# q, k and v handed over feature-on-partitions: no transposes of them on the chip, and a new order of the front

## The chip, the cores and the metric

One core of a Trainium2 chip runs the whole program. The metric is device time in microseconds (us), the median of several runs. TensorE (PE) does the matrix products, VectorE (DVE), ScalarE (ACT) and GpSimd (POOL) the elementwise work, SyncE (SP) issues every load and store from one queue.

## The reference, cut to what matters

```python
# q, k, v: (2, 8, 576, 64) float32; w_in 512x1024, w_out 1024x512, w1, w2: four experts; inputs of w_* are float64
mask_plain = (rel >= 0) & (rel < 32)                              # heads 0-3
mask_dil = (rel >= 0) & (rel < 128) & (rel % 4 == 0)              # heads 4-7
attn = softmax(where(mask, q @ k.T / 8, -1e9)); x = (attn @ v) as (1152, 512)
h = x @ w_in; solu = h * softmax(h); x = layernorm(solu) * g_ln @ w_out
out = sum over 4 experts of p[:, e] * (relu(x @ w1[e]) @ w2[e])
```

## The kernel before, in words

The program has two parts. The **front** computes the attention and the first layer; its order is written out as a table of tokens, `ORDER`, and each token runs a Python generator to its next `yield`, so the table sets the order of instructions on every engine (a `+` moves the step's copy or subtraction to another engine). The **loop** behind the table computes the experts and is the same for all kernels here.

The tokens of the front:

- `lI`, `VI`: load of a 128-row block of `w_in` (float64, as pairs of integers) and its conversion to a high and a low float32 part (`convert`, `conv_in`), five or six steps on ACT, DVE and POOL; `lO`, `VO` the same for `w_out`.
- `lD`, `lP`: loads of q and k with positions on partitions, for the dilated heads (4-7) and the plain heads (0-3). `AD`, `AP` (`att_AD`, `att_AP`): TensorE transposes of them into PSUM and copies to `qTd`, `kTd`, `qTp`, `kTp`, with features on partitions. `lvd`, `lvp` load v.
- `UD`, `UP` (`att_U`): a unit of attention, 96 positions of four dilated heads or 192 of four plain ones; three units of each kind for each of two batches, so twelve. In a unit PE writes mask and scores (L307, L318), DVE and ACT do the softmax, PE transposes the probabilities (L343), a copy brings them to `pt`, PE multiplies with v (L357), and a copy and a subtraction write the result's high and low parts `xhi`, `xlo`.
- `H.t` (`moe_H`): token tile t (0 to 8) times `w_in`, 24 matmuls of 512 columns in one go (L386), then the softmax-like function; `T.t` (`moe_T`) transposes its result (L413); `X.c.dp` (`moe_X`) multiplies a third of the tokens with half of `w_out`, 48 matmuls (L433).
- `WP`, `XQ`, `WV`: preparation of the experts' weights and inputs by additions and high/low splits; `u`, `d` the first products of the experts (L545, L615).

PSUM has four tiles: `pm` (two buffers; for `H`, `X` and most of `AD`, `AP`) and `pa` (two; for the units and `T`). The queue of each engine is executed in order, so a waiting instruction holds what stands behind it.

Of the kernel before, what the change touches and what calls it, by code (L numbers as in the profile page):

```python
# [8 lines left out]
F32 = mybir.dt.float32  # L9
BF16 = mybir.dt.bfloat16  # L10
# [37 lines left out]
def fused_kernel(ctx, tc, q, k, v, w_in, w_out, g_ln, probs, w1, w2, out):  # L48
    nc = tc.nc
    B, H, S, D = q.shape  # L50
# [45 lines left out]
    warmb = ap1.tile([128, 224], BF16, name="warmb", tag="warmb")
    nc.vector.memset(warmb, 0.0)
    nc.vector.memset(kTd[:, :, 0:32], 0.0)
    nc.vector.memset(kTp[:, :, 0:32], 0.0)
    nc.vector.memset(vd[0:32, 0], 0.0)  # L100
# [29 lines left out]
    def load_qk(quad, u, b):  # L130
        for nm, src in (("q", q), ("k", k)):
            if quad == "D":
                h0 = 4 + 2 * u
                t = rdp.tile([72, 2, 8 * D], F32, name=f"rd{nm}", tag=f"rd{nm}")
                nc.sync.dma_start(out=t, in_=src[b, h0:h0 + 2].rearrange("h (p r) d -> p h (r d)", r=8))
            else:
                s0 = TH * u
                t = ap2.tile([96, 2, 4, D], F32, name=f"rp{nm}", tag=f"rp{nm}")
                nc.sync.dma_start(out=t, in_=src[b, 0:4, s0:s0 + TH].rearrange("h (p r) d -> p r h d", r=2))
            raws[nm, quad, u, b] = t  # L140

    def load_vd(b):
        vr = v[b, 4:8].rearrange("h (i r j) d -> r i h (j d)", r=2, j=2)
        for c in range(3):
            x = max(96 * c - 32, 0)
            while x < 96 * c + 96:
                r, i = divmod(x, 144)
                n = min(144 - i, 96 * c + 96 - x)
                p = x - (96 * c - 32)
                nc.sync.dma_start(out=vd[p:p + n, c], in_=vr[r, i:i + n])  # L150
                x += n
# [14 lines left out]
    fill = [0]  # L166

    def busy(ps):
        for _ in range(fill[0]):
            nc.tensor.matmul(ps[:, 1, 288:512], lhsT=warmb[:, 0:128], rhs=warmb, start=True, stop=True)  # L170
# [87 lines left out]
    qT = {}  # L258
    cnt = [0]

    def att_AD(u, b):
        if ("D", b) not in qT:
            qT["D", b] = ap1.tile([128, 4, S // 2], F32, name="qTd", tag="qTd")
        for nm, dst in (("q", qT["D", b]), ("k", kTd[:, :, 32:])):
            raw = raws.pop((nm, "D", u, b))
            pa = ptile(True)
            busy(pa)
            for rp in range(4):
                for hd in range(2):
                    o = 144 * hd + 72 * (rp % 2)  # L270
                    nc.tensor.transpose(pa[:, rp // 2, o:o + 72], raw[:, hd, 2 * D * rp:2 * D * rp + 2 * D], ident[:72, :72])
            yield
            copy(dst[:, 2 * u:2 * u + 2].rearrange("d h (x e) -> d e h x", e=2), pa[:, :, 0:288].rearrange("d e (h x) -> d e h x", h=2))
            if nm == "q":
                yield

    def att_AP(t, b):
        qt = ap2.tile([128, 2, TH], F32, name="qTp", tag="qTp")
        qT["P", t, b] = qt
        s0 = TH * t  # L280
        for nm, dst in (("q", qt), ("k", kTp[:, :, 32 + s0:32 + s0 + TH])):
            pa = ptile(b == 0)
            busy(pa)
            raw = raws.pop((nm, "P", t, b))
            for hp in range(2):
                for r in range(2):
                    o = (2 * hp + r) * 96
                    nc.tensor.transpose(pa[:, 0, o:o + 96], raw[:, r, 2 * hp:2 * hp + 2].rearrange("p j d -> p (j d)"), ident[:96, :96])
            yield
            copy(dst.rearrange("d h (p r) -> d h r p", r=2), pa[:, 0, 0:384].rearrange("d (h r p) -> d h r p", h=2, r=2))  # L290
            if nm == "q":
                yield
# [461 lines left out]
```

## Time and profile before

| | before |
|---|---|
| median of 3 runs | 562.73 us (561.83 to 563.07) |
| the profiled execution | 561.9 us |
| its span, first to last instruction | 560.1 us |
| busy share of the span | PE 95%, DVE 65%, ACT 35%, POOL 34% |
| moved by DMA | 35.79 MB |

The profile divides the span into stretches and tells how long each engine was busy in each. A busy PE is one with a matmul in flight, not one at its peak.

### The profile page before, as it was taken

The page shows a single profiled execution, that of the slowest core. Times are in us where ns is not written, and L with a number is a line of the kernel's source. Part 1 is how long each engine was busy: PE and PEld are TensorE (multiplying, and loading weights), DVE is VectorE, ACT ScalarE, POOL GpSimd, SP SyncE. Part 2 cuts the span into 40 slices and gives each one's busy share as a digit, 9 for nine tenths or more (in the row PEclk, how much of TensorE's full clock was granted, in tenths as well). Part 3 has the DMA queues.
Part 4 walks back from the last instruction along what each step waited for, and adds up shares of the span by engine and source line. Part 5 has one row for each costly group of instructions (what it writes and reads, how often), then busy time and mean ns, then how long its engine had stood idle before and what let it go on. Part 6 is the DMA issues. An engine that isn't in the chain of part 4 may idle for free.

```text
span 560.1 us, 9023 instructions
## 1 busy us (share of the span) xinstructions
PE 533.2 (95%) x3772; PEld 479.6 (86%) x3772; DVE 365.1 (65%) x472; ACT 197.5 (35%) x309; POOL 191.6 (34%) x143
## 2 busy tenths in 40 slices
PE   2888989999999899999999999999999999999997
PEld 1667877988999889898898989989889898998986
DVE  4997889617579988476558547537645854854542
ACT  3666666415325234142142223214224322321300
POOL 3463131000063463074147127307413812730300
PEclk9999999999999999999999999999999999999999
DMA  8984262000023500040030003004004000100022
GB/s 250 286 212 112 85 158 57 1 1 1 1 77 96 179 27 1 0 152 0 1 133 18 1 19 132 1 1 151 2 1 133 18 1 4 72 0 1 1 75 94
DMA packets 33944, 35.79 MB, mean 64 GB/s; under 512 B 18800, under 2 KB 21872, under 8 KB 33520
## 3 DMA queue, kind: packets, MB, share of 16 engines
q1 hardware_dynamic: 33904, 35.22, 21.1%
q8 instruction: 29, 0.48, 0.3%
q14 instruction: 11, 0.09, 0.1%
HBM read 32.86 MB, written 2.36 MB: 63 GB/s over the span
## 4 chain that ended last, share of the span: by engine, by line
PE 84%; DVE 8%; ACT 3%; issue 2%; DMA 1%; SPq 1%; DVEq 0%; ACTq 0%
PE pa L615 18%; PE pm L615 17%; PE pm L545 15%; PE pa L545 15%; PE pm L386 9%; PE pm L433 6%; PE pa L357 2%; DMA draw<-in_moe_w_in_dram 1%; PE pa L413 1%; DVE xol L464 1%; PE pa L343 1%; PE pa L318 1%; DVE hl L464 1%; ACT pt L184 1%; DVE cva L206 1%
## 5 line engine op out<-in xcount | busy, mean ns | idle before, releaser
L558 DVE SCALAR_TENSOR_TENSOR hl<-ct,hh 128x512 fp32r<-128x512 f32 (+1 forms) x64 | 63.2, 1005 | 33.3 <-ACT hh L556 33.2
L556 ACT ACTIVATE hh<-ct 128x512 fp32r<-128x512 f32 (+1 forms) x64 | 42.2, 682 | 59.7 <-DVE ct L588 29.7
L545 PE MATMUL pm<-xoh,hh 128*128 128x256 f32 (+1 forms) x192 | 56.9, 296 | 1.1 <-DVE ct L588 1.1
L615 PE MATMUL pm<-wh,hh 128*128 128x512 f32 (+1 forms) x148 | 56.9, 384 | 0.6 <-DVE xf L620 0.6
L545 PE MATMUL pm<-xol,hh 128*128 128x256 f32 (+1 forms) x192 | 56.9, 297 | 0.3 <-DVE xol L464 0.3
L545 PE MATMUL pa<-xoh,hh 128*128 128x256 f32 (+1 forms) x192 | 56.9, 296 | 0.0
L545 PE MATMUL pa<-xoh,hl 128*128 128x256 f32 (+1 forms) x192 | 56.8, 296 | 0.0
L545 PE MATMUL pm<-xoh,hl 128*128 128x256 f32 (+1 forms) x192 | 56.8, 296 | 0.0
L545 PE MATMUL pa<-xol,hh 128*128 128x256 f32 (+1 forms) x192 | 56.8, 296 | 0.0
L615 PE MATMUL pm<-wl,hh 128*128 128x512 f32 (+1 forms) x148 | 56.8, 384 | 0.0
L615 PE MATMUL pm<-wh,hl 128*128 128x512 f32 (+1 forms) x148 | 56.7, 383 | 0.0
L615 PE MATMUL pa<-wh,hh 128*128 128x512 f32 x144 | 56.2, 390 | 0.1
L615 PE MATMUL pa<-wl,hh 128*128 128x512 f32 x144 | 56.1, 390 | 0.0
L615 PE MATMUL pa<-wh,hl 128*128 128x512 f32 x144 | 56.0, 389 | 0.0
L464 POOL TENSOR_TENSOR wl<-wl,wh 128x1024 fp32r<-128x1024 f32 x8 | 19.3, 2412 | 96.6 <-ACT wh L184 95.4
L620 DVE SCALAR_TENSOR_TENSOR xf<-pm,pr,xf 128x512 f32<-128x512 f32 (+1 forms) x33 | 24.1, 730 | 32.9 <-PE pm L615 32.9
L620 DVE SCALAR_TENSOR_TENSOR xf<-pa,pr,xf 128x512 f32<-128x512 f32 x31 | 23.1, 745 | 29.4 <-PE pa L615 29.4
L184 ACT CAST wh<-wl 128x1024 fp32r<-128x1024 f32 x15 | 15.8, 1053 | 71.0 <-PE pa L615 40.6
L464 POOL TENSOR_TENSOR hl<-sw,hh 128x512 fp32r<-128x512 f32 x20 | 30.4, 1520 | 27.8 <-ACT hh L184 27.8
L545 PEld LDWEIGHTS pm<-xoh,hh 128*128 128x128 f32 x192 | 36.4, 190 | 1.6 <-issue 1.3
L572 POOL TENSOR_TENSOR ct<-ct,ct 128x512 f32<-128x512 f32 (+1 forms) x15 | 22.3, 1484 | 45.0 <-ACT ct L570 45.0
L545 PEld LDWEIGHTS pm<-xol,hh 128*128 128x128 f32 x192 | 36.4, 190 | 0.8 <-DVE xol L464 0.5
(219 smaller groups left out, 1323.3 us busy)
## 6 DMA issues: line engine op xcount, KB each, us to landing
wl<-in_moe_w_dram SPq DMA_DIRECT2D x16, 512.0 KB, 3.9
cvr<-in_moe_w_out_dram SPq DMA_DIRECT2D x8, 512.0 KB, 3.7
rw<-in_moe_w_dram SPq DMA_DIRECT2D x8, 512.0 KB
wh<-in_moe_w_dram SPq DMA_DIRECT2D x8, 512.0 KB, 6.0
draw<-in_moe_w_in_dram SPq DMA_DIRECT2D x3, 1024.0 KB, 8.6
out_dram<-xf SPq DMA_DIRECT2D x8, 256.0 KB, 2.0
vp<-in_v_dram SPq DMA_DIRECT2D x10, 128.0 KB, 3.8
rpq<-in_q_dram SPq DMA_DIRECT2D x6, 192.0 KB, 7.1
```

Source lines behind the costliest of these rows:

```text
L184: nc.scalar.copy(out, in_)
L206: pick().tensor_tensor(out=au, in0=au, in1=low.bitcast(U32), op=ALU.add)
L357: nc.tensor.matmul(po[64 * row:64 * row + 64, 0, o:o + 96], lhsT=vv, rhs=pt[:, j, :, g, :], start=True, stop=True)
L386: nc.tensor.matmul(pm[:, n, :], lhsT=xx[:, kk, cols], rhs=ww["in", kk][:, 512 * n:512 * n + 512], start=(kk == 0 and i < 2), stop=(kk == K ...
L433: nc.tensor.matmul(pm[:, dd, 0:CW], lhsT=w_, rhs=x_[:, f, :], start=(f == 0 and i == 0), stop=(f == KF - 1 and i == 2))
L464: pick().tensor_tensor(out=out, in0=a, in1=b, op=op)
L545: nc.tensor.matmul(ps[:, ff, 0:n], lhsT=a[:, kk, fc], rhs=b[:, kk, :], start=kk == 0 and m == 0, stop=kk == 1 and m == 2)
L556: nc.scalar.activation(out=hv, in_=src, func=AF.Relu)
L558: nc.vector.scalar_tensor_tensor(out=lv, in0=src, scalar=0.0, in1=hv.bitcast(F32), op0=ALU.max, op1=ALU.subtract)
L572: poolv().tensor_tensor(out=c12, in0=c21, in1=c22, op=ALU.add)
L615: nc.tensor.matmul(po[:, u, 0:dn], lhsT=h_[:, f, cols], rhs=w_, start=(f == 0 and i == 0), stop=(f == 3 and i == 2))
L620: nc.vector.scalar_tensor_tensor(out=acc[:, t, dc], in0=po[:, u, 0:dn], scalar=pr[:, t, e:e + 1], in1=acc[:, t, dc], op0=ALU.mult, op1=ALU ...
```

## The change: layouts from outside, and what is done with the time

The host now hands over q and k with 128 partitions of features (two heads, or two of four interleaved positions, times 64) as `qp`, `kp`, `qd`, `kd`, and v with all heads of a position in one row as `vp`, `vd`. `att_AD` and `att_AP` are gone with their transposes and copies; the loads write `qTp`, `kTp`, `qTd`, `kTd` directly. These tiles and `vd` exist twice now, one set for each batch. `moe_H` yields after each quarter (the first two tiles), half or whole of its matmuls (`HCUT`), and `moe_X` after a half or the whole (`XCUT`), with its two output blocks interleaved, so that the table can put units between the pieces. The table `ORDER` is another one throughout. The computation, the loop behind the table and the number of matmuls of every kind beside the transposes of q and k are unchanged.

```diff
+KORD = (0, 1, 2, 3)
+HCUT = (1, 1, 2, 2, 4, 2, 4, 4, 4)
+XCUT = (2, 2, 4)
 ORDER = """
-lI.0 VI.0 lI.3 VI.0 lP.0.0 lD.1.0 AP.0.0 AP.0.0 VI.0 AD.1.0 VI.3 VI.3 lI.4 VI.3 AP.0.0 VI.3 VI.4 VI.4 lD.0.0 VI.3 AP.0.0 lP.1.0 lI.1 UP.0.0 AD.1.0
+lI.0 lP.0.0 VI.0 VI.0 VI.0 UP.0.0 lI.1 lD.0 VI.0 lI.4 VI.1 UP.0.0 UP.0.0 lP.1.0 UD.0.0 VI.0 VI.1 VI.1 UP.1.0 VI.1 VI.0+ VI.4 UP.0.0 VI.4 UD.0.0 UD.0.0
...
+    for b, p in enumerate((erp, ap1)):
+        kTp.append(p.tile([128, 2, 32 + S], F32, name=f"kTp{b}", tag=f"kTp{b}"))
...
+    def load_qk(quad, t, b):
+        if quad == "D":
+            nc.sync.dma_start(out=qTd[b], in_=qd[b])
+            nc.sync.dma_start(out=kTd[b][:, :, 32:], in_=kd[b])
+        else:
+            s0, s1 = (0, TH) if t == 0 else (TH, S)
+            nc.sync.dma_start(out=qTp[b][:, :, s0:s1], in_=qp[b, :, :, s0:s1])
+            nc.sync.dma_start(out=kTp[b][:, :, 32 + s0:32 + s1], in_=kp[b, :, :, s0:s1])
...
-    def att_AD(u, b):
...
-    def att_AP(t, b):
...
-        for kk in range(KD):
+        for n_, kk in enumerate(KORD):
...
+            if n_ % HCUT[t] == HCUT[t] - 1:
+                yield
...
+        for j in range(KF // 2):
+            for f in (2 * j, 2 * j + 1):
+                for dd in range(2):
...
+            if j % XCUT[c] == XCUT[c] - 1:
+                yield
```

The queue of SP at the start of the program. Before, behind a half block of `w_in` (0.52 MB), stands this; `draw` is a block of `w_in`, `rpq`, `rdq` are raw q, `rpk`, `rdk` raw k:

```order
L218 DMA draw_180<-in_moe_w_in_dram 128x1024
L139 DMA rpq<-in_q_dram 96x8x64
L139 DMA rpk<-in_k_dram 96x8x64
L135 DMA rdq<-in_q_dram 72x2x512
L135 DMA rdk<-in_k_dram 72x2x512
L214 DMA draw_175<-in_moe_w_in_dram 128x512
L135 DMA rdq<-in_q_dram 72x2x512
L135 DMA rdk<-in_k_dram 72x2x512
L139 DMA rpq<-in_q_dram 96x8x64
L139 DMA rpk<-in_k_dram 96x8x64
L218 DMA draw_234<-in_moe_w_in_dram 128x1024
```

After, behind the same half block and the first third of `qTp` and `kTp` of batch 0 (0.20 MB each):

```order
L206 DMA draw_216<-in_moe_w_in_dram 128x1024
L135 DMA qTd_107<-in_qd_dram 128x1152
L136 DMA kTd_104<-in_kd_dram 128x4x288
L202 DMA draw_180<-in_moe_w_in_dram 128x512
L139 DMA qTp_106<-in_qp_dram 128x2x384
L140 DMA kTp_103<-in_kp_dram 128x2x384
L206 DMA draw_310<-in_moe_w_in_dram 128x1024
L155 DMA vp<-in_vp_dram 96x256
L155 DMA vp<-in_vp_dram 128x256
L144 DMA vd_105<-in_vd_dram 96x512
L144 DMA vd_105<-in_vd_dram 128x512
L206 DMA draw_409<-in_moe_w_in_dram 128x1024
```

The last block of `w_in` (`draw_409`) is the fifteenth load and ends 7.24 MB; before, the last one is the seventeenth and ends 6.98 MB.

PE around the first tile of `H`. Before, the tile is one run of 24 matmuls (twelve such rows of two), of which the first stand here:

```order
L343 MATMUL pa<-ident,pd_111 128x128 x6
L357 MATMUL pa<-pt,vd 64x96 x8
L271 MATMUL pm<-ident,rdk 128x72 x8
L357 MATMUL pa<-pt,vd 64x96 x8
L288 MATMUL pm<-ident,rpq 128x96 x4
L386 MATMUL pm<-wh_177,xhi 128x512 x2
L386 MATMUL pm<-wl_178,xhi 128x512 x2
L386 MATMUL pm<-wh_177,xlo 128x512 x2
L386 MATMUL pm<-wh_418,xhi 128x512 x2
```

After, the first two quarters stand further up (each between steps of units), and the last two are these (`wh_377`, `wh_443` are the third and fourth block of `w_in`); the first quarter of tile 1 follows directly:

```order
L269 MATMUL pa<-kTd_109,qTd_112 32x64 x24
L336 MATMUL pm<-wh_377,xhi 128x512 x2
L336 MATMUL pm<-wl_378,xhi 128x512 x2
L336 MATMUL pm<-wh_377,xlo 128x512 x2
L258 LDWEIGHTS identb
L258 MATMUL pa<-mask,identb 128x192
L258 LDWEIGHTS identb
L258 MATMUL pa<-mask,identb 128x192
L269 MATMUL pa<-kTp_108,qTp_111 32x64 x24
L336 MATMUL pm<-wh_443,xhi 128x512 x2
L336 MATMUL pm<-wl_444,xhi 128x512 x2
L336 MATMUL pm<-wh_443,xlo 128x512 x2
```

The transposes L271 and L288 are gone, and the scores of two units of batch 1 (`kTd_109`, `kTp_108`) now stand ahead of the last two quarters. In all, eight mask-and-score groups, four groups of six probability transposes and four groups of products with v stand ahead of the fourth quarter; before, five, three and three stand ahead of the first.

POOL where the experts' operands are prepared (`XQ` and `WP`). Before:

```order
L464 TENSOR_TENSOR xol<-xf,xoh 128x4x256
L464 TENSOR_TENSOR ct_1810<-xf 128x2x256
L464 TENSOR_TENSOR hl<-sw_1817,hh 128x512
L464 TENSOR_TENSOR hl<-rw_1803,hh 128x512 x2
L572 TENSOR_TENSOR ct_1972<-ct_1970,ct_1971 128x2x256
L464 TENSOR_TENSOR xol<-sw_1963,xoh 128x2x320
L464 TENSOR_TENSOR wl_2042<-wl_1957,wh_2041 128x1024
L464 TENSOR_TENSOR xol<-xf,xoh 128x2x320
L464 TENSOR_TENSOR sw_1965<-xf,sw_1963 128x640
```

After:

```order
L417 TENSOR_TENSOR ct_1744<-xf 128x2x256
L417 TENSOR_TENSOR sw_1677<-rw_1616 128x2x256
L417 TENSOR_TENSOR xol<-ct_1744,xoh 128x2x256
L417 TENSOR_TENSOR ct_1745<-xf,ct_1743 128x2x256
L417 TENSOR_TENSOR w7l<-sw_1677,w7h 128x512
L417 TENSOR_TENSOR sw_1678<-rw_1618,sw_1676 128x2x256
L417 TENSOR_TENSOR sw_1799<-xf 128x640
L417 TENSOR_TENSOR sw_1801<-xf 128x640
L417 TENSOR_TENSOR hl<-rw_1618,hh 128x512
L417 TENSOR_TENSOR sw_1802<-xf,sw_1800 128x640
```

Other steps of the preparation went to POOL, among them two more differences of 640 columns (`sw<-xf`), and some subtractions of low parts went back to DVE.

## Rows read from the trace of the kernel before

**Rows 1.** Busy time of each engine in stretches of the span (us and count; granted clock, DMA share, GB/s).

```profile
0.00:40.00 40.00, 23.88 (x385) 19.24 (x386) 29.73 (x52) 21.71 (x33) 18.88 (x33) 1.00 0.93 256
40.00:107.00 67.00, 61.97 (x752) 52.30 (x750) 57.05 (x95) 42.77 (x74) 17.41 (x16) 1.00 0.37 90
107.00:151.00 44.00, 43.82 (x258) 39.64 (x259) 21.69 (x31) 15.46 (x24) 0.00 (x0) 1.00 0.00 1
151.00:163.00 12.00, 12.00 (x77) 12.00 (x76) 5.48 (x10) 5.54 (x8) 4.53 (x4) 1.00 0.26 89
163.00:195.00 32.00, 30.60 (x206) 29.80 (x204) 31.11 (x34) 10.48 (x17) 15.80 (x8) 1.00 0.34 109
195.00:206.00 11.00, 10.57 (x50) 8.78 (x51) 8.59 (x11) 6.37 (x11) 7.03 (x5) 1.00 0.18 68
206.00:557.00 351.00, 350.38 (x2052) 317.81 (x2050) 210.96 (x242) 95.15 (x146) 127.95 (x80) 1.00 0.12 40
```

The columns behind the length are PE, PE's weight loads, DVE, ACT, POOL.

**Rows 2.** The chain that ended last, in order of time, around the first `H` (start, us, what).

```profile
5.28 8.34 DMA draw<-in_moe_w_in_dram
...
37.73 1.23 DVE cva L206
38.95 0.68 DVE kTd L182
...
39.68 2.33 PE pm L386 x9
```

**Rows 3.** PE's timeline: one group of each step of a unit, late in the front, and one early (start, us, line, operation, count).

```profile
26.20 1.54 PE L343 MATMUL pa<-ident,pd 128*128 128x128 f32 x6 [0.27 <-POOL pd L337]
...
76.19 0.82 PE L343 MATMUL pa<-ident,pd 128*128 128x128 f32 x6
76.97 0.33 PE L307 MATMUL pa<-mask,identb 128*128 128x192 bf16 x2
77.22 0.73 PE L318 MATMUL pa<-kTd,qTd 64*32 64x64 f32 x48
77.89 0.93 PE L357 MATMUL pa<-pt,vd 128*64 128x96 f32 x16
```

**Rows 4.** The same chain, a tile of `H` and a pair of output blocks of `X` without a stall.

```profile
108.72 8.52 PE pm L433 x48
117.25 5.49 PE pm L386 x24
```

**Rows 5.** Busy time of PE with the plain heads' transposes (L288) alone, and then with the dilated heads' (L271), up to 107.

```profile
0.00:39.60 39.60, 4.02 (x20) 2.86 (x20) 1.00 0.93 257
39.60:107.00 67.40, 3.56 (x28) 2.88 (x28) 1.00 0.37 90
...
0.00:39.60 39.60, 6.33 (x48) 5.72 (x48) 1.00 0.93 257
39.60:107.00 67.40, 1.39 (x16) 1.18 (x16) 1.00 0.37 90
```

**Rows 6.** Loads in the first 40 us, all engines, in the same columns as rows 1 (the last number is GB/s).

```profile
0.00:10.00 10.00, 0.88 (x4) 0.61 (x4) 4.43 (x15) 2.71 (x4) 4.97 (x23) 1.00 0.80 247
10.00:20.00 10.00, 6.84 (x91) 6.25 (x92) 7.49 (x8) 6.40 (x10) 2.60 (x2) 1.00 0.98 281
20.00:30.00 10.00, 7.79 (x175) 5.59 (x175) 8.52 (x17) 7.26 (x13) 5.47 (x5) 1.00 1.06 261
...
28.00:32.00 4.00, 3.12 (x25) 2.90 (x26) 3.77 (x6) 2.38 (x4) 3.17 (x3) 1.00 0.98 217
```

**Rows 7.** The steps of one conversion of a 128x1024 block, from the timelines of ACT, DVE and POOL.

```profile
26.61 1.15 ACT L200 ACTIVATE eva<-draw 128x1024 f32<-128x1024 f32 x1
29.29 1.12 ACT L198 ACTIVATE draw<-draw 128x1024 int32<-128x1024 uint32 x1
37.71 1.07 ACT L184 CAST wh<-eva 128x1024 fp32r<-128x1024 f32 x1
...
35.45 0.65 DVE L202 TENSOR_SCALAR cva<-cva 128x1024 uint32<-128x1024 uint32 x1
36.48 1.22 DVE L204 SCALAR_TENSOR_TENSOR cva<-draw,cva 128x1024 uint32<-128x1024 uint32 x1
...
32.28 2.40 POOL L206 TENSOR_TENSOR eva<-eva,draw 128x1024 uint32<-128x1024 uint32 x1
38.85 2.41 POOL L231 TENSOR_TENSOR wl<-eva,wh 128x1024 fp32r<-128x1024 f32 x1 [4.17 <-ACT wh L184]
```

**Rows 8.** A DVE row beside a POOL row, and the same DVE row alone later (timelines).

```profile
16.83 2.43 DVE L202 TENSOR_SCALAR cva<-cva 128x512 uint32<-128x512 uint32 x1
46.59 0.42 DVE L202 TENSOR_SCALAR cva<-cva 128x512 uint32<-128x512 uint32 x1
...
16.37 2.36 POOL L231 TENSOR_TENSOR wl<-eva,wh 128x1024 fp32r<-128x1024 f32 x1 [9.73 <-DMA rdk<-in_k_dram]
```

**Rows 9.** Preparation of the experts: two DVE rows of one form, and what POOL did meanwhile or takes for a difference of 640 columns (timelines).

```profile
163.27 2.76 DVE L464 TENSOR_TENSOR hl<-rw,hh 128x512 fp32r<-128x512 f32 x1
169.48 0.69 DVE L464 TENSOR_TENSOR hl<-sw,hh 128x512 fp32r<-128x512 f32 x1
...
162.89 2.60 POOL L464 TENSOR_TENSOR xol<-xf,xoh 128x1024 fp32r<-128x1024 f32 x1 [0.54 <-ACT xoh L184]
199.47 2.16 POOL L464 TENSOR_TENSOR sw<-xf,sw 128x640 f32<-128x640 f32 x1
```

More of the change, by code (lines that the diff above doesn't have):

```diff
@@ L45, with fused_kernel @@
+XQ.1 XQ.1+ XQ.1 u.1 u.1 WV.0+ u.1 u.1 XQ.1 WP.1+ u.1 d.1 WP.1 WP.1 WP.1 WP.1+ d.0 d.2 u.1 WP.1+ d.0 d.2 d.1 WP.1+ u.1 u.1 WP.1+ u.1 u.1 u.1 u.1+ u.1
+u.1 d.3 WP.1+ WP.1 lV.1 WP.1+ u.1 WP.1 u.1 u.1 u.1 d.3 WP.1 u.1 WP.1+ u.1 u.1 WP.1 WP.1 WP.1 u.1 WP.1+
 """
 @with_exitstack
-def fused_kernel(ctx, tc, q, k, v, w_in, w_out, g_ln, probs, w1, w2, out):
+def fused_kernel(ctx, tc, qp, kp, qd, kd, vpd, vdd, w_in, w_out, g_ln, probs, w1, w2, out):
     nc = tc.nc
-    B, H, S, D = q.shape
+    B, _, _, S = qp.shape
+    D = 64
@@ L87, in fused_kernel @@
     early = ExitStack()
-    rdp = early.enter_context(tc.tile_pool(name="rdp", bufs=2, side="right"))
     erp = early.enter_context(tc.tile_pool(name="erp", bufs=1, side="right"))
-    kTp = ap1.tile([128, 2, 32 + S], F32, name="kTp", tag="kTp")
-    kTd = ap1.tile([128, 4, 32 + S // 2], F32, name="kTd", tag="kTd")
-    vd = ap1.tile([128, 3, 4, 2 * D], F32, name="vd", tag="vd")
+    kTp, kTd, vd, qTp, qTd = [], [], [], [], []
+    for b, p in enumerate((erp, ap1)):
+        kTp.append(p.tile([128, 2, 32 + S], F32, name=f"kTp{b}", tag=f"kTp{b}"))
+        kTd.append(p.tile([128, 4, 32 + S // 2], F32, name=f"kTd{b}", tag=f"kTd{b}"))
+        vd.append(p.tile([128, 3, 4, 2 * D], F32, name=f"vd{b}", tag=f"vd{b}"))
+        qTp.append(p.tile([128, 2, S], F32, name=f"qTp{b}", tag=f"qTp{b}"))
+        qTd.append(p.tile([128, 4, S // 2], F32, name=f"qTd{b}", tag=f"qTd{b}"))
     pds = [ap1.tile([128, 2, 480], F32, name=f"pd{i}", tag=f"pd{i}") for i in range(3)]
     sms = [ap1.tile([128, 6, 65], F32, name=f"sm{i}", tag=f"sm{i}") for i in range(3)]
[L96 to L100, printed above, removed]
+    for b in range(2):
+        nc.vector.memset(kTp[b][:, :, 0:32], 0.0)
+        nc.vector.memset(kTd[b][:, :, 0:32], 0.0)
+        nc.vector.memset(vd[b][0:32, 0], 0.0)
     identb = ap1.tile([128, 128], BF16, name="identb", tag="identb")
@@ L125, in fused_kernel, with load_vd @@
     nc.gpsimd.memset(mhalf, -0.5)
-    raws = {}
     vps = {}
[L130 to L151, printed above, removed]
+    def load_qk(quad, t, b):
[6 more added lines that the diff above has]
+            nc.sync.dma_start(out=kTp[b][:, :, 32 + s0:32 + s1], in_=kp[b, :, :, s0:s1])
+    def load_vd(c, b):
+        p = 32 if c == 0 else 0
+        nc.sync.dma_start(out=vd[b][p:128, c].rearrange("p h d -> p (h d)"), in_=vdd[b, 96 * c - 32 + p:96 * c + 96])
     def load_vp(u, b):
@@ L161, in load_vp @@
                 p, x = 32, 0
-            nc.sync.dma_start(out=t[p:128, cc], in_=v[b, 0:4, x:x + 128 - p].rearrange("h p d -> p h d"))
+            nc.sync.dma_start(out=t[p:128, cc].rearrange("p h d -> p (h d)"), in_=vpd[b, x:x + 128 - p])
     whi, wlo = {}, {}
     alt = [False]
[L166 to L170, printed above, removed]
     late = [False]
@@ L256, in lo_psum @@
             nc.vector.tensor_tensor(out=lo, in0=ps, in1=hi.bitcast(F32), op=ALU.subtract)
-    qT = {}
-    cnt = [0]
-    def att_AD(u, b):
[L262 to L275, printed above, removed]
-    def att_AP(t, b):
[L278 to L292, printed above, removed]
     unit = {}
     for b in range(B):
-        for quad, t in (("D", 0), ("P", 0), ("D", 1), ("D", 2), ("P", 1), ("P", 2)):
+        for quad, t in (("P", 0), ("D", 0), ("D", 1), ("P", 1), ("D", 2), ("P", 2)):
             unit[quad, t, b] = len(unit)
@@ L300, in att_U @@
         ps = ptile(False)
-        busy(ps)
         if quad == "D":
-            qt, kt, mi = qT["D", b], kTd, (1, 2, 0)[t]
+            qt, kt, mi = qTd[b], kTd[b], (1, 2, 0)[t]
         else:
-            qt, kt, mi = qT.pop(("P", t, b)), kTp, 3 if t == 0 else 0
+            qt, kt, mi = qTp[b][:, :, TH * t:TH * t + TH], kTp[b], 3 if t == 0 else 0
         for j in range(2):
@@ L348, in att_U @@
         po = ptile(False)
-        busy(po)
         vt = None if quad == "D" else vps.pop((t, b))
@@ L738 @@
     nc = _bacc.Bacc("TRN2", target_bir_lowering=False, num_devices=1)
+    inputs = _lay_out(inputs)
     arrays, args = {}, []
```

75 lines of the change are left out of this document (38 added, 37 removed).

## The prediction

> **What bounds the kernel now.** I read the busy time by stretches first. From 206 us on PE is busy 350.4 of 351 us [rows 1]; the change leaves that loop as it is, so nothing can come from there. PE is also full from 107 to 163 (55.8 of 56). It loses time in three places: 16.1 us before 40, 5.0 between 40 and 107, 1.4 and 0.4 in the two stretches from 163 to 206. A busy PE is not a useful one, though: the three steps of the change that touch it lie among its busy rows.
>
> The chain that ended last says what the first 40 us wait for: a load of `w_in`, then conversion steps on DVE, and at the end the copy of a `kTd` transpose that frees a `pm` tile, on which the first `H` starts at 39.68 [rows 2]. DVE is nearly full there and behind it: 29.7 of 40, 57.1 of 67. From 163 to 195 it is the limit outright, 31.1 of 32 [rows 1].
>
> **How I count.** The end of the front is the sum of PE's useful work (units, `H`, `T`, `X`), which the change does not alter, and of what PE loses. So I compare the losses up to two moments and see what is lost behind them. Prices at full speed, late in the front [rows 3]: mask and scores 0.33 + 0.73 = 1.06 us, six probability transposes 0.8, the products with v 0.9; a tile of `H` 5.5, so 1.37 a quarter [rows 4]. The early six transposes took 1.54 at a granted clock that reads 1.00 (2.4 GHz) in every stretch; whatever slowed them is part of the early loss.
>
> **Before.** Ahead of 39.7 stand five score groups, three of transposes and three of products (the rows of the order): 5 x 1.06 + 3 x 0.8 + 3 x 0.9 = 10.4 us useful, so 29.3 lost. Behind it, transposes of q and k are 28 + 16 rows, busy 3.56 + 1.39 = 4.95 [rows 5]. Rows overlap at their edges by about a tenth, some 0.1 us in each of nine groups, so 4.1 is the other end; I take 4.5. Those ahead of 39.6 (4.02 + 6.33) are inside the 29.3 already and must not be counted again. Idle behind: 5.0.
>
> **After, the start.** The fourth quarter of `H.0` needs the last block of `w_in`. It ends 7.24 MB of loads, before 6.98. With the rates of the first three stretches of 10 us (247, 281, 261 GB/s [rows 6]) 5.28 MB are in at 20 us and the rest needs 7.5: it lands at 27.5, before at 26.5. The larger runs of the new layouts might raise the rate; I take no gain for it. The conversion costs 1.12 + 1.15 on ACT, 0.65 + 1.22 on DVE, 2.40 on POOL, 1.07 on ACT, 2.41 on POOL [rows 7], 10.0 together: 37.5 without a queue. But on DVE it stands behind 52 rows, about 25 us by the durations of such rows now and most of them tied to data that comes from 9 us on, so its two steps end at about 34 rather than at 31.6, and the low part is there at about **40**. PE has by then, in its order, eight score groups, four of transposes, four of products and three quarters of `H.0` behind it, and two matmuls of the fourth: 8.5 + 3.2 + 3.6 + 4.1 + 0.5 = 19.9 us useful, 20.1 lost. That is **9.2 less** than before. The price has two ends. Without the queue it is 37.5 (gain 11.7). At the slowest 4 us of the early loads (217 GB/s) the block lands at 4 + 6.7/0.217 = 35, the low part at 45 to 47, and as the scores ahead wait for loads too, 2 to 4 us are left.
>
> **After, behind that.** No transposes: **4.5 less**. Twenty copies of them go, 17 from ACT and 3 from DVE; DVE also sheds two copies of `pt` and takes three multiplications to `pd` from POOL. I count some 4 us less on it up to the last unit, 82 instead of 86.8. They are no gain by themselves, since ACT is 64% busy there, but they let the units come earlier. PE's order has `H` and `X` in about eight more pieces; a piece starts with a pair of matmuls 0.1 us longer than the others: **0.8 more**. The idle 5.0 stays as it is: I follow the order through two tiles and find DVE one or two instructions ahead of PE each time. From below it would be 0.2, as PE shows between 107 and 151; from above 11, if every unit waits half a microsecond twice.
>
> **The rest at nothing.** Three more memsets on DVE stand where it waits for the first load. The doubled tiles of batch 0 are freed where `w_out` is to be converted, so its first step on ACT waits for batch 0's last product; before, it waited for the raw tiles in the same place, and 25 us of `w_out` conversion lie ahead of the first `X` in both. If ACT stands there, `pt` copies queue behind it: 0 to 2 us. The matmuls behind the last `T` are the same 144 of `X`, 25 us, in both orders, and under them the same preparation runs; its 1.8 us of idle PE stay.
>
> **Sum.** 9.2 + 4.5 - 0.8 = 12.9; a few tenths for queues I could not follow, so 12.4. The profiled execution took 561.9 (span 560.1); it becomes 549.5. The median of the runs is 0.8 above that execution, so I predict **550.2**.
>
> **A rule that speaks against it.** A DVE row of 0.42 us took 2.43 because a POOL row ran beside it until 18.73; it ended 0.5 us behind that [rows 8]. The change gives POOL three conversions of 1024 columns early, 3 x 2.4 = 7.2 us, where it had one such and one of half the size, 3.6 by columns. The Trainium skill (SBUF — State Buffer, Who interferes with whom) says that the two engines share a pair of ports which one instruction holds entire, the other waiting. The row agrees; by the rule alone up to 3.6 us more of DVE's early rows would be blocked, and the sum would be 553.8.
>
> **The rivals.** *DVE becomes the limit.* Up to the last unit it has 82 us of work and stood idle for 20 of 107; PE would be there at 31 + 27 + 17 + 2.4 = 77.4 useful (twelve units, five tiles of `H`, two of `X`, three of `T`) plus 26 lost, at 103. DVE with its old idle time is there at 102: no room. Blocked rows as in [rows 8], or waits for PE of as long as before, would put it at 106 to 108, and the front ends 4 to 6 us later: 554 to 556. For it: 57 of 67 us. Against: ACT and PE serve it earlier. *The loads are late.* The scores of two units of batch 1 now stand ahead of the third and fourth quarter, so PE, in order, waits for loads that end 8.7 and 9.6 MB into the queue. At 261 GB/s they are in at 33 and 36.5, in time; at 217 at 42 and 46: gain 6 to 8, 554 to 556. Against: only one stretch of 4 us was that slow. *The quarters give nothing*, since the first `H` is bound by the conversion as before, and only the later transposes pay: 4.5 - 0.8, so 559. Against: the work in front of it grows by 9 us all the same. *Better:* with the conversion at 37.5 and 2 us less idle, 545.5.
>
> *Slower than before.* It could only be the preparation from 163 to 195, where DVE has 0.9 us free. POOL takes two more differences of 640 columns, 2.16 each [rows 9], and a DVE row beside POOL took 2.76 instead of 0.69. One such block costs 2.1 us, and PE stands once the 1.8 us are used up. To lose 12.4 and 1.1 more, seven more blocks would be needed on the way to the first products, with one more POOL row in all. I do not see them.
>
> **Chances.** My forecast, 547.5 to 553: 0.56. DVE, ports or loads, 553 to 557: 0.21. The quarters give nothing, 557 to 561.5: 0.07. Better than 547.5: 0.12. Slower: 0.03; within 0.2%, about what this measurement can tell from no change: 0.01. The range that holds 8 in 10 leaves out the best tenth and the last two cases: 546 to 557.
>
> **What would show it.** In the profile after: no row with a raw tile of q or k; the first `H` row near 27 to 30 and its fourth quarter near 40, with the scores of batch 1 ahead of it; PE's idle time before 40 still large but the busy rows useful; idle about 5 us from there to the last product with v, which ends near 100 to 104 instead of 108.7; the last `T` group 12 us earlier than 150.8; from there on the same distances as before, and 351 us of loop. A wait of PE on DVE in the units' rows would make the first rival right, a wait on `qTd` or `kTp` loads the second, more than 3 us of idle PE in the 45 us ahead of the loop the last.

## The result, and the profile after

| | before | after |
|---|---|---|
| median, us | 562.9 (561.8 to 563.3, 4 runs) | 547.98 (546.9 to 550.0, 4 runs) |
| ratio | | 0.974, interval 0.971 to 0.977 |
| profiled execution (span), us | 561.9 (560.1) | 548.3 (546.5) |

The span fell by 13.6 us where 12.4 was forecast. One execution of a later kernel, the one with the transposes put back, took 875.0 us at a mean granted clock of 0.568 and is in none of the numbers here. Busy time of each engine in stretches, in the columns of [rows 1], the stretches cut at the same places of the program:

```profile
0.00:40.00 40.00, 21.53 (x453) 16.02 (x454) 32.90 (x63) 21.98 (x31) 20.85 (x33) 0.96 0.88 299
40.00:95.00 55.00, 53.96 (x588) 45.50 (x588) 48.65 (x84) 41.24 (x65) 13.28 (x13) 1.00 0.24 78
95.00:138.00 43.00, 43.00 (x259) 38.60 (x258) 23.42 (x27) 14.74 (x22) 0.00 (x0) 1.00 0.00 1
150.00:182.00 32.00, 28.85 (x195) 28.12 (x194) 25.99 (x25) 12.76 (x19) 23.34 (x14) 1.00 0.42 132
193.00:544.00 351.00, 349.76 (x2048) 317.19 (x2046) 210.49 (x240) 96.14 (x147) 129.25 (x81) 1.00 0.12 40
```

PE stands for 1.0 us between 40 and 95, where it stood for 5.0 in the stretch that answers to it (40 to 107 before), and for 3.15 between 150 and 182 (before: 1.4 from 163 to 195). The loop is as it was. On PE's timeline the four quarters of `H.0` begin at 27.07, 30.13, 38.88 and 41.70, the last product with v and the last `T` group at 97.34 and 136.15:

```profile
27.07 0.71 PE L336 MATMUL pm<-wh,xhi 128*128 128x512 f32 x2
...
30.13 0.71 PE L336 MATMUL pm<-wh,xhi 128*128 128x512 f32 x2
...
36.18 1.44 PE L307 MATMUL pa<-pt,vp 128*64 128x96 f32 x16 [1.83 <-issue]
...
38.88 1.12 PE L336 MATMUL pm<-wh,xhi 128*128 128x512 f32 x2
...
41.70 0.73 PE L336 MATMUL pm<-wh,xhi 128*128 128x512 f32 x2
...
97.34 0.88 PE L307 MATMUL pa<-pt,vp 128*64 128x96 f32 x16
...
136.15 1.91 PE L364 MATMUL pa<-ident,e 128*128 128x128 f32 x16
```

The last product ends at 98.2, 10.5 us earlier than the 108.7 of [rows 4] and ahead of the 100 to 104 that were forecast; the last `T` group comes 14.6 earlier than at 150.79; behind it 1.05 us are given back (409.3 us from there to the end of the span before, 410.35 now). What PE waits for from 0 to 195 (us in total, times, the longest):

```profile
PE pa L258 <- POOL mhalf L129: 7.7, 1, 7.7
PE pa L269 <- DMA kTd<-in_kd_dram: 3.8, 1, 3.8
PE pa L269 <- DMA kTp<-in_kp_dram: 2.7, 1, 2.7
PE pa L307 <- issue: 1.8, 1, 1.8
PE pa L498 <- DVE ct L535: 1.6, 1, 1.6
...
PE pm L498 <- DVE ct L529: 1.3, 1, 1.3
```

The first three lie ahead of 27 us, when masks and loads are not there yet. The fourth, 1.8 us at 34.4, and the two waits for `ct` in the preparation of the experts are the places that the experiments turn to.

### The profile page after: what moved, and what is told of

Same layout as the page of the kernel before. It is cut to its first block, busy times and chain, and to the rows that moved or that the text cites. A ratio compares the mean times of both kernels' runs of the same rounds, so it can differ in the third digit from the quotient of the medians.

```text
span 546.5 us, 8746 instructions
## 1 busy us (share of the span) xinstructions
PE 520.1 (95%) x3660; PEld 467.0 (85%) x3660; DVE 361.4 (66%) x465; ACT 194.8 (36%) x296; POOL 196.6 (36%) x145
## 4 chain that ended last, share of the span: by engine, by line
PE 86%; DVE 5%; POOL 2%; DMA 2%; issue 2%; ACT 1%; SPq 1%; DVEq 0%; POOLq 0%; ACTq 0%
PE pm L568 18%; PE pa L568 18%; PE pm L498 15%; PE pa L498 15%; PE pm L336 9%; PE pm L385 5%; DMA draw<-in_moe_w_in_dram 2%; PE pa L307 2%; PE pa L294 1%; PE pa L364 1%; PE pa L269 1%; DVE xol L417 1%; DVE hh L170 1%; POOL sw L417 1%; POOL ct L417 0%
## 5 line engine op out<-in xcount | busy, mean ns | idle before, releaser
L568 PE MATMUL pm<-wh,hh 128*128 128x512 f32 (+1 forms) x148 | 56.9, 384 | 0.6 <-DVE xf L573 0.6
L568 PE MATMUL pm<-wl,hh 128*128 128x512 f32 (+1 forms) x148 | 56.8, 384 | 0.0
L568 PE MATMUL pm<-wh,hl 128*128 128x512 f32 (+1 forms) x148 | 56.7, 383 | 0.0
L568 PE MATMUL pa<-wl,hh 128*128 128x512 f32 x144 | 56.1, 390 | 0.0
L568 PE MATMUL pa<-wh,hh 128*128 128x512 f32 x144 | 56.1, 390 | 0.0
L568 PE MATMUL pa<-wh,hl 128*128 128x512 f32 x144 | 56.0, 389 | 0.0
L525 POOL TENSOR_TENSOR ct<-ct,ct 128x640 f32<-128x640 f32 (+1 forms) x15 | 22.1, 1475 | 46.2 <-ACT ct L523 42.2
L498 PEld LDWEIGHTS pa<-xoh,hh 128*128 128x128 f32 x192 | 36.4, 190 | 2.1 <-issue 1.8
## 6 DMA issues: line engine op xcount, KB each, us to landing
draw<-in_moe_w_in_dram SPq DMA_DIRECT2D x3, 1024.0 KB, 10.4
```

Of the source, the lines that this page charges most:

```text
L498: nc.tensor.matmul(ps[:, ff, 0:n], lhsT=a[:, kk, fc], rhs=b[:, kk, :], start=kk == 0 and m == 0, stop=kk == 1 and m == 2)
L525: poolv().tensor_tensor(out=c12, in0=c21, in1=c22, op=ALU.add)
L568: nc.tensor.matmul(po[:, u, 0:dn], lhsT=h_[:, f, cols], rhs=w_, start=(f == 0 and i == 0), stop=(f == 3 and i == 2))
```

## The experiments

All times stand beside 547.98 of the changed kernel and about 562.4 of the kernel before. "Idle" is PE's idle time.

**The layouts alone.** The changed kernel with the sequence of before:

```
-HCUT = (1, 1, 2, 2, 4, 2, 4, 4, 4)
-XCUT = (2, 2, 4)
+HCUT = (4,) * 9
+XCUT = (4, 4, 4)
...
-lI.0 lP.0.0 VI.0 VI.0 VI.0 UP.0.0 lI.1 lD.0 VI.0 lI.4 VI.1 UP.0.0 UP.0.0 lP.1.0
...
+lI.0 VI.0 lI.3 VI.0 lP.0.0 lD.0 VI.0 VI.3 VI.3 lI.4 VI.3 VI.3 VI.4 VI.4 VI.3
...
```

> The new layouts with the order of the kernel before: its transposes and copies dropped from the sequence, one load per batch for qd and kd, H and X in one piece each, the release of the early tiles put behind the last product of batch 0 that reads them. Theory (the order brings the larger part, since PE's early loss before the first H hangs on the conversion of w_in and not on the transposes): first H at 36 to 39 us as before (the loads run faster by some 10%, which is 1 to 2 us), transposes behind it 4.1 to 5 less, so 554 to 558. Rival (taking the transposes and copies away is the gain, the order a polish): 547 to 551, first H near 30.

It took 556.4 us (ratio 0.989, 0.986 to 0.992), as its theory said: some 6 us are the layouts, and 8.4 the new order on top of them. Two of its stretches, and then two rows of PE's timeline:

```profile
0.00:40.00 40.00, 18.82 (x324) 13.98 (x324) 30.29 (x55) 18.86 (x26) 20.35 (x33) 1.00 0.75 261
40.00:95.00 55.00, 50.06 (x660) 41.01 (x659) 49.65 (x83) 35.26 (x60) 15.88 (x16) 1.00 0.33 105
```
```profile
37.05 1.22 PE L336 MATMUL pm<-wh,xhi 128*128 128x512 f32 x2
...
102.07 1.54 PE L307 MATMUL pa<-pt,vp 128*64 128x96 f32 x32 [0.39 <-DVE pt L170]
```

The first `H` comes at 37.05, 2.6 earlier than in [rows 2], and from there to the last product 66.6 us pass where 69.0 did: so the transposes and copies behind the first `H` were worth 2.5 us. The idle time between 40 and 95 is 4.9; before the change it was 4.7 in the same stretch.

**Every `H` in one piece** (the changed sequence, the matmuls of a tile at the place of its last piece), then **only `H.0`**, then **all but `H.0`**:

```
+            pend.append((n_, kk, seq))
+            if n_ == KD - 1:
+                for m_, k_, sq in pend:
...
```

In the second kernel the tile waits for its last piece only where `t == 0`, in the third the condition is `t == 0 or n_ == KD - 1`.

> The changed kernel with all matmuls of an H tile issued at the place of its last piece; nothing else moves. Theory: the three early quarters of H.0, 4.1 us of PE, stood in time in which PE would have been idle; collected they come behind the conversion's end at 41.6, so 551 to 553 (4 more, with a few tenths less for the pieces that are saved). Rival one: PE was late at the fourth quarter by itself, so whatever is moved is made up behind it: 547 to 549. Rival two: other units' work fills the early gap in the order that then stands, half the price: 550.

> The changed kernel with the three early quarters of H.0 moved back to the place of its fourth, all other pieces as they are. It divides the 11 us that the kernel with every H in one piece lost. Theory: 4.1 us of PE's work leaves the early gap, so the fourth quarter's end comes 3.5 to 4.5 later, plus up to 2 for a lower granted clock between 28 and 36 us, and the rest of the 11 belongs to the later pieces, under which the units' chains of DVE and ACT run: 551.5 to 554. Rival: the early quarters are all of it, since the units behind them come late in turn: 557 to 560.

> The changed kernel with H.0 in its quarters, and H.1, H.2, H.3 and H.5 in one piece each at the place of their last piece: the complement of the kernel with only H.0 in one piece, which lost 4.1 us and kept 1.04 us of idle PE between 40 and 95. Theory (the later pieces stand over the units' chains on DVE and ACT; whole tiles leave PE idle between them, as before the change): idle time between 40 and 95 goes from 1.0 to 4 to 6, the fourth quarter stays at 40 to 42, 551 to 555. Rival (those pieces are only overhead, 0.1 us each, and the 4.4 us of idle time of the kernel with every H whole followed from its late start): idle near 1, 547 to 548.5.

They took 559.1 (ratio 0.994), 552.1 (0.982) and 553.9 (0.986). The first missed its forecast of 551 to 553 by 6 us; the other two, which were to divide the loss, fell where their theories put them: 4.1 us for the early quarters, 6.0 for the later pieces, together 10.1 of the 11.1. Some of this is granted clock, which fell in some executions of a kernel and not in others. Between the executions whose mean clock reads 1.00 (0.999 in the third kernel) the early quarters are worth 3.1 to 4.0, the later pieces 5.5 to 6.3, and both 9.0 to 10.5. In the profile of the second kernel the last `T` group stands at 137.90, 2.1 and 2.8 later than in two kernels with the changed front whose clock held (135.15 and 135.78, below); the rest of its loss comes behind that, and in the executions with a lower clock. The stretch from 40 to 95 in the three:

```profile
40.00:95.00 55.00, 49.54 (x530) 40.88 (x512) 40.60 (x67) 33.95 (x55) 13.09 (x13) 0.94 0.20 69
```
```profile
40.00:95.00 55.00, 53.96 (x541) 45.52 (x540) 46.78 (x79) 39.96 (x64) 12.49 (x13) 1.00 0.24 78
```
```profile
40.00:95.00 55.00, 49.61 (x509) 41.34 (x508) 44.95 (x76) 37.28 (x59) 11.82 (x13) 0.97 0.24 78
```

Two of PE's waits in the third, from 40 to 100:

```profile
PE pa L294 <- DVE xlo L244: 1.7, 1, 1.7
PE pa L307 <- ACT pt L172: 1.3, 1, 1.3
```

Idle 5.5, 1.0 and 5.4: it comes back with the whole tiles behind 40, whatever `H.0` does. PE then waits for the units' chains, as the two waits show, 3.0 of the 5.4 us. A piece of 1.4 to 2.7 us of `H` between the scores and the transposes of a unit is what covers its steps on DVE and ACT; 5.5 us in one lump covers one unit and leaves the next bare. So I read these waits; no run moved a single piece. The kernel with every `H` whole also lost granted clock, in the profile at two places, one of them here:

```profile
24.00:28.00 4.00, 2.62 (x64) 1.69 (x60) 3.83 (x8) 3.43 (x5) 2.28 (x3) 1.00 1.06 390
28.00:32.00 4.00, 2.77 (x22) 2.17 (x22) 3.97 (x7) 3.67 (x5) 1.78 (x2) 0.59 1.05 376
32.00:36.00 4.00, 3.94 (x72) 3.25 (x72) 3.19 (x5) 1.75 (x3) 2.05 (x2) 0.56 0.77 164
```

**The transposes back**, without copies:

```
+        if b == 1 and (quad, t) in (("D", 1), ("P", 1), ("D", 2), ("P", 2)):
+            for _ in range(7):
+                nc.tensor.transpose(ps[:, 1, 288:360], ident[:72, :], ident[:72, :72])
+            for _ in range(4):
+                nc.tensor.transpose(ps[:, 1, 288:384], ident[:96, :], ident[:96, :96])
```

> The changed kernel with 44 transposes of the identity (28 with 72 partitions, 16 with 96) put ahead of the scores of four units of batch 1, into the unused half of their score tile; nobody reads them, so no copies come with them. These are as many and of the shapes that stood behind the first H before. Theory (PE is full from 40 on, each matmul there is on the path): 4.1 to 5.0 us more, 552 to 553. Rival (the units wait for DVE anyway, so the transposes lie in PE's gaps, of which there is 1.0 us left between 40 and 95): 548 to 549.5.

It took 550.1 to 551.7 (ratio 0.979, 0.976 to 0.982), the profiled span is 2.7 above that of the changed kernel. Neither forecast holds: the work is on the path, but it is smaller. One of the four groups, and the mask that follows it:

```profile
59.00 0.60 PE L259 MATMUL pa<-ident 72*128 72x72 f32 x7
59.44 0.49 PE L261 MATMUL pa<-ident 96*128 96x96 f32 x4
59.77 0.33 PE L263 MATMUL pa<-mask,identb 128*128 128x192 bf16 x2
```

From start to start eleven transposes take 0.77 to 0.83 us, 3.2 for all 44, and 0.4 of that goes into idle time (0.66 left between 40 and 95). The run had the two counts the wrong way about ([rows 5] has 28 of the plain heads' form, with 96 partitions, and 16 of the other); by the same rows, 0.063 and 0.083 each, the right mixture is 3.3.

**The old tail**, the sequence of before from the scales on:

```
-X.1.0 sc T.7+ T.8 endH lW.0 T.7 X.2.1 X.1.1 WP.0+ X.2.0 endX lV.0 WP.0 XQ.0 XQ.0+ WP.0+
...
+X.1.0 sc endH T.7+ T.7 lW.0 X.1.1 T.8 XQ.0 WP.0+ WP.0+ WP.0 WP.0+ XQ.0 XQ.0 XQ.0+
...
```

> The changed kernel's order up to the scales, and from there on the order that the kernel before had (which engine splits what included; the pieces of X that are over at that point dropped). PE waits 3.1 us for ct tiles between 150 and 182 in the changed kernel, 1.8 in the same stretch of before. Theory one (the new tail's division put 23.3 us on POOL instead of 15.8, and DVE rows beside POOL rows last 2 us): the waits go back to about 1.8, 546.3 to 547. Rival (the tail is DVE's sum whatever the division, and it comes 14 us earlier, when DVE is no freer): 548 to 551.

545.6 us (545.2 to 545.7; ratio 0.969, 0.967 to 0.971), the fastest of all. Of the 2.8 us of span, 1.0 is made ahead of the tail (below, on the clock) and 1.8 in it. The stretches of the changed kernel, and then of this one:

```profile
150.00:160.00 10.00, 10.00 (x60) 10.00 (x59) 5.39 (x7) 3.09 (x5) 6.57 (x6) 1.00 0.00 0
170.00:182.00 12.00, 8.85 (x61) 8.12 (x61) 11.96 (x13) 3.11 (x6) 7.98 (x4) 1.00 0.45 148
```
```profile
150.00:160.00 10.00, 10.00 (x60) 10.00 (x59) 9.28 (x12) 3.33 (x6) 4.81 (x3) 1.00 0.00 0
170.00:182.00 12.00, 11.23 (x69) 9.94 (x68) 11.27 (x14) 4.09 (x7) 5.03 (x3) 1.00 0.51 175
```

In the changed kernel DVE is busy for 5.4 of the first 10 us. It waits twice for an `xoh` of ACT: for 2.2 us, while ACT's queue stands at a copy that waits for `X` on PE, and for 2.4, while it stands at a cast that waits for a result of POOL. It then has no moment free when PE's products need it at 170; with the old division it does 9.3 us of the work while PE is covered by `X`.

**Three POOL rows less in the tail**, at their old places, and in a second kernel with `WV.0` (its fourth step) moved up, right behind the eighth step of `XQ.1`. The sequence at the three places, the plus taken off:

```
-XQ.1 u.0 XQ.1+ XQ.1 WP.0+
+XQ.1 u.0 XQ.1 XQ.1 WP.0+
...
-u.1 u.1 XQ.1 XQ.1+ XQ.1 u.1 u.1 WV.0+ u.1 u.1
+u.1 u.1 XQ.1 XQ.1 XQ.1 u.1 u.1 WV.0 u.1 u.1
```

> The changed kernel with three of its rows of the preparation on DVE instead of POOL, at the same places of the sequence: the differences XQ.1 9 and XQ.1 14 (640 columns, 0.8 on DVE) and the split WV.0 4 (1024 columns, 1.2 on DVE). Theory (in the changed kernel ct at L525 took 2.05 instead of 0.68 and xol 2.40 instead of 0.81 since these POOL rows ran beside them, and PE's waits of 1.3 and 1.6 for ct come from that): both rows fall to 0.7 and 0.8, PE's waits shrink to under 1, the time falls by 1.5 to 2.5, to 545.5 to 546.5. Rival (DVE's sum is the limit there, and 2.8 us more of work on it is no better than blocked rows): no change or up to 2 us slower, 547.5 to 550.

> The kernel with three POOL rows less (the differences XQ.1 9 and 14 and the split WV.0 4 on DVE), with one thing mended: there WV.0 4 stood on DVE at its old place of the sequence, ended at 186, and PE waited 4.2 us for wl; here it stands right behind XQ.1 8, about 8 us earlier. Theory (POOL rows beside DVE rows made the changed kernel's 3.1 us of waits in the tail; the misplaced row alone made the 4 us lost): no wait for wl, none above 0.6 for ct, 545.3 to 546.8. Rival (DVE's sum is the limit): the waits come back for other tiles, 547.5 to 549, no faster than the changed kernel.

551.9 us (0.982), outside both forecasts, and 547.0 (0.972, 0.970 to 0.974). Two DVE rows of the changed kernel and the POOL row beside the second:

```profile
172.19 2.05 DVE L525 TENSOR_TENSOR ct<-ct,ct 128x512 f32<-128x512 f32 x1
...
174.76 2.40 DVE L417 TENSOR_TENSOR xol<-sw,xoh 128x640 fp32r<-128x640 f32 x1
...
173.65 2.84 POOL L417 TENSOR_TENSOR wl<-wl,wh 128x1024 fp32r<-128x1024 f32 x1
```

The same two DVE rows in the first of the two kernels, and the split; then the wait for it:

```profile
171.45 0.68 DVE L525 TENSOR_TENSOR ct<-ct,ct 128x512 f32<-128x512 f32 x1
...
172.65 0.81 DVE L417 TENSOR_TENSOR xol<-sw,xoh 128x640 fp32r<-128x640 f32 x1
...
184.75 1.22 DVE L417 TENSOR_TENSOR wl<-wl,wh 128x1024 fp32r<-128x1024 f32 x1
```
```profile
PE pa L568 <- DVE wl L417: 4.2, 1, 4.2
```

So the blocked rows are what the theory said, 2.05 becomes 0.68 and 2.40 becomes 0.81 once POOL is quiet, and the waits for `ct` of L529 and L535 are gone. But POOL had run `WV.0` far ahead of its place in the sequence, since its queue was short; on DVE it waited its turn, and PE for it. Behind that wait the granted clock read 0.56 and 0.59 in the two stretches of 4 us from 184, so a part of the 3.9 us is clock. With the split moved up one wait of 2.3 us is left of the 3.1 (L568, for the `ct` of L547), and DVE, with 2.8 us more to do, is busy for 11.8 of the 12 us from 170 to 182: half of the theory, half of the rival. The 0.9 us beside the changed kernel lie within that kernel's own spread; in the profiles the time behind the last `T` group is 1.0 us shorter (409.4). The rule of the Trainium skill (SBUF — State Buffer, Who interferes with whom) agrees with these rows; how much it costs is decided by the order of the queues.

**POOL's additions on DVE at the start** (`VI.1`, `VI.2`, `VI.3`, step 5):

```
-UP.0.0 VI.1+ VI.4
+UP.0.0 VI.1 VI.4
...
-UP.2.0 VI.2+ UP.1.0
+UP.2.0 VI.2 UP.1.0
...
-UP.1.0 VI.3+ UD.1.0
+UP.1.0 VI.3 UD.1.0
```

> The changed kernel with the last addition of the conversion of three w_in blocks (1, 2 and 3, 1024 columns) on DVE instead of POOL, the same places of the sequence. It prices the blocked rows against the work: in the changed kernel DVE rows of 1.80, 1.69 and 1.42 beside POOL rows lost 3.3 us up to 42. Theory (POOL's share is worth it, DVE is busy 33 of 40 us): three DVE rows of about 1.3 come in, 3.9, and 2 to 2.5 of blocked time go; the fourth quarter stays within 1 us, the end 0 to 2 us later, 547.5 to 550. Rival (the ports bound the start): the fourth quarter 1.5 to 3 us earlier, 545 to 546.5.

551.7 us (0.981), 3.7 slower, more than the forecast. A row of 1.42 us beside POOL fell to 0.70, but the third and fourth quarters came at 40.61 and 44.34, since PE waits 3.0 us for an `xlo` that frees a tile of scores:

```profile
PE pa L258 <- DVE xlo L244: 3.0, 1, 3.0
```
```profile
35.54 1.22 DVE L194 CUSTOM_DVE_ANT_0 cva<-draw,cva 128x2048 uint16<-128x2048 uint16 x1
```

The second row is the addition of `VI.2`. It ended on DVE at 36.76, where POOL had ended it at 32.71. ACT's queue stood 2.4 us for it, and behind the cast that waited stands the `xhi` from which this `xlo` is made. So the blocked rows at the start were the cheaper side.

**A filler in the gap at 34 us, and DVE's order there.**

```
+        if (quad, t, b) == FILL[0]:
+            for _ in range(FILL[1]):
+                nc.tensor.matmul(last[0][:, 1, 288:480], lhsT=identb, rhs=mask[:, 0].rearrange("p c k -> p (c k)"), start=True, stop=True)
```
```
-UP.2.0 VI.3 VI.3 UP.2.0 UP.1.0 UD.1.0 UP.2.0 VI.2+ UP.1.0 VI.2 UD.1.0
+UP.2.0 UP.2.0 UP.1.0 UD.1.0 UP.2.0 VI.3 VI.3 VI.2+ UP.1.0 VI.2 UD.1.0
...
-UP.1.0 VI.3+ UD.1.0
+UP.1.0 VI.3 UD.1.0
...
-VO.0.1 VI.3+ UP.2.0
+VO.0.1 VI.3 UP.2.0
```

> The changed kernel with eleven more matmuls of the mask (192 columns, whose result nobody reads) in front of the products of unit P.1 of batch 0, where PE stood 1.8 us in the profile (34.3 to 36.2) and the granted clock then fell to 0.57 for 4 us. Theory (the clock falls because PE stands there; the fall costs 1.0 to 1.4 us in those executions that have it): granted clock 1.00 in every stretch of the profile, mean clock 1.0 in every execution, all within 546.5 to 547.7. Rival (the fall has nothing to do with this gap): means of 0.994 to 0.997 in some, times up to 550 as before. The added work itself lies in the gap and costs 0 to 0.3.

> The changed kernel with the old tail, and two edits at the start, around 34 us, where PE stood 1.8 us for the subtraction L279 (the tile of scores comes free for the products by it) while DVE did two conversion steps of w_in block 3: those two steps (0.7 to 1.4 and 1.2) come behind that maximum and subtraction, and the block's last addition and its low part are made on DVE (1.25 each) instead of POOL (2.4 each), so the block is ready no later. Theory (PE waits for DVE's order there, not for DVE's work): the gap falls under 0.6, the fourth quarter comes 1.2 to 1.8 earlier, 543.7 to 544.6 beside 545.6. Rival one (the fourth quarter then waits for the conversion): 545.2 to 545.8. Rival two (2.5 us more on DVE delay the units behind): 546 to 547.5.

The filler missed its aim: it waited for the same DVE row as the products, the gap stayed at 1.8 us, and 548.2 us (0.975) is no change. The eleven matmuls then took 1.07 us behind the gap. The mean clock reads 1.000 in all four executions, as the theory had it, but with PE standing as long as before this says nothing about the gap; it reads so in all four of the kernel with the old tail too, and in two of four of the changed kernel. Its wait names what the profile of the changed kernel calls "issue" (L282 is this kernel's line for the subtraction, L279):

```profile
PE pa L304 <- DVE sm L282: 1.8, 1, 1.8
```

The second kernel, made on the one with the old tail, took 548.6 (0.975), 3 us slower than that. The gap at 34.4 fell to 0.3, as its theory said, and PE then stood 3.0 at the next place, on its timeline and in the stretches:

```profile
38.83 0.50 PE L258 MATMUL pa<-mask,identb 128*128 128x192 bf16 x2 [3.02 <-DVE xlo L244]
```
```profile
36.00:38.00 2.00, 0.00 (x0) 0.00 (x0) 2.00 (x4) 0.35 (x2) 1.05 (x1) 0.97 0.64 178
38.00:40.00 2.00, 1.17 (x50) 0.86 (x50) 2.00 (x4) 1.62 (x3) 0.62 (x1) 0.50 0.10 35
```

`xlo` is now what stands behind the conversion, and the fourth quarter came at 44.27 instead of 40.51. The mechanism is that of rival two: DVE is full from 34 to 40 (2.0 of 2 us in the last rows), and one wait of PE was exchanged for another. Its price was too low; the granted clock fell behind the new gap (0.50 in the last row). The new order and the 2.5 us more on DVE were not run apart, so what the order alone would do is not shown.

## Why the prediction was right, step by step

**PE's loss up to the fourth quarter: 9.2 forecast, 7.0 measured.** By the same count 19.4 us of useful work stand ahead of 41.70 (without two matmuls of the quarter), so 22.3 are lost against 29.3. That the early quarters fill time in which PE would stand is shown: with `H.0` in one piece 3 to 4 us come back. Three steps of the working were off. I took no gain from larger runs, and the loads came in much faster, 6.35 MB by 20 us instead of 5.28 [rows 6]:

```profile
0.00:10.00 10.00, 1.81 (x52) 1.08 (x52) 6.50 (x20) 2.49 (x3) 5.76 (x23) 1.00 0.75 273
10.00:20.00 10.00, 2.50 (x99) 1.77 (x100) 7.85 (x13) 5.26 (x7) 3.63 (x2) 1.00 1.05 362
20.00:30.00 10.00, 9.17 (x155) 6.89 (x156) 9.39 (x18) 7.23 (x11) 5.76 (x5) 1.00 1.03 370
```

The last block of `w_in` landed at 25.6 in the trace (issued at 15.16, 10.4 us before), not at 27.5. It gave nothing in itself, since the block's first step ran on ACT at 28.64 and its low part was ready at 41.6 instead of 40: the queues of ACT and DVE set that date. Nor was it that date for which the quarter waited. PE ran without a wait from 36.18 on and came to the low part 0.7 us after POOL had written it:

```profile
39.16 2.41 POOL L219 TENSOR_TENSOR wl<-eva,wh 128x1024 fp32r<-128x1024 f32 x1 [2.11 <-ACT wh L172]
...
42.27 0.62 PE L336 MATMUL pm<-wl,xhi 128*128 128x512 f32 x2
```

The quarter came late by PE's own queue: PE had stood 1.8 us at 34.4 for DVE, behind which the granted clock fell to 0.57 in this execution. In the kernel with the old tail the front is the same, the clock held, and the fourth quarter came at 40.51: 8.2. There PE reached the low part just as it was ready, at 41.1.

**Transposes behind the first `H`: 4.5 forecast, 3.2 to 3.3 measured** on PE, 2.5 to 3.0 in time. This term was mis-sized, below its lower end of 4.1: I added the busy times of rows that overlap, where the distance from start to start is the price.

**Idle time behind 40: 5.0 kept as it was, and it fell to 1.0.** With the 0.2 of the next stretch that is 4.2 us of gain where I had none. This is the step that failed. I followed the old and the new order for DVE being ahead of PE, and took the pieces of `H` for overhead of 0.8; the kernels with whole tiles show that they are what closes PE's gaps (idle 5.4 to 5.5 without them). Their own 0.1 us a pair is in the rows (0.71 and 0.62), but no sum here is fine enough to show it.

**The tail: nothing forecast, 1.3 lost.** I saw that POOL got two more differences and priced a block at 2.1 us, then let it go under 1.8 us of idle time. PE's idle time from 150 to 193 is 3.15 instead of 1.8, and the old tail takes 1.8 us of span back. The mark that I had set for the rival that ends slower, more than 3 us of idle PE there, was just reached; its mechanism came, at a tenth of the price that it needed.

Sum: 7.0 + 3.2 + 4.2 - 1.3 = 13.1 of the 13.6. That the forecast of 12.4 was so near is luck in good part: 2.2 + 1.3 too much on two terms and 1.3 in the tail, 4.8 together, stood against 4.2 + 0.8 too little. The rivals: DVE as the limit did not come (48.7 of 55 us, ACT and PE served it earlier). Late loads did not either: PE waited 3.8 us for `kTd` and 2.7 for `kTp`, the sign that I had named, but up to 17.4 us, for units of batch 0; the loads of batch 1 made no wait. The quarters were worth 3 to 4. The rule that speaks against the change holds row by row, but the early rows beside POOL cost less than the work would on DVE.

## What to carry to other kernels

Price an inserted operation by the distance from start to start, and cut a long matmul tile into pieces where other chains wait in between: here that gave some 6 us behind 40 and 3 to 4 ahead of it. When a front is made faster, look at the order behind it again; and before a row is moved to another engine, look where its old queue really ran it, which may be far ahead of its place in the program. Where one engine is full, a new order of its queue may only move the wait, as in the one case tried here.

## What the runs showed of the hardware

The loads in packets, before and after:

```profile
DMA packets 33944, 35.79 MB, mean 64 GB/s; under 512 B 18800, under 2 KB 21872, under 8 KB 33520
```
```profile
DMA packets 20247, 35.78 MB, mean 65 GB/s; under 512 B 3568, under 2 KB 8368, under 8 KB 19824
```

With the same bytes in fewer and larger packets the loads of 10 to 30 us rose from 281 and 261 to 362 and 370 GB/s; in the kernel with the layouts alone and the old sequence the stretch from 10 to 20 reads 400. The Trainium skill (DMA: Bandwidth & Descriptors, Specifications) asks for 512 B per transfer at the full rate, and the trace agrees. The order of the loads changed as well, and what the small packets alone cost was not measured apart.

The granted clock fell to its lower level of 1.2 GHz for some 3 to 7 us at a time, behind places where PE had stood. Behind the gap of 3.0 us (two kernels) every execution's mean clock was below 0.998. Behind the gap of 1.8 at 34 us it fell in four profiles (0.58 and 0.56 from 36 to 40 in the changed kernel's) and held at 1.00 in four others with a gap as long, among them those with the old tail and with the filler. Shorter gaps did it too: in the kernel with every `H` whole PE had stood 0.8 and then 1.0 us ahead of the 0.59 from 28 to 32. At 34 us the fall cost 1.0 us: from the second quarter of `H.0` to the last `T` group 106.0 us pass in the changed kernel (30.13 to 136.15) and 104.9 in the one with the old tail, whose clock held (30.25 to 135.15). What decides whether it falls was not settled; the filler that was to show it stood behind the gap instead of in it.
